# Output rows of one batch of an attention and routing kernel: transposed by DMA instead of on TensorE

## The chip, the core and the metric

One core of a Trainium2 chip runs the whole kernel. The metric is device time in microseconds (us). The core has five engines with instruction streams of their own, each worked through in order: TensorE (PE in the rows; its weight loads are listed apart as PEld), VectorE (DVE), ScalarE (ACT), GpSimd (POOL) and SyncE (SP). Engines wait for one another by semaphores. 16 DMA engines move data between HBM and SBUF, and can also move it from SBUF to SBUF.

## The reference

```python
# q, k, v: (8, 12, 448, 64) float32
scores = (1 / sqrt(64)) * q @ k.T
attn   = maximum(scores, 0) ** 2 / 448
x      = (attn @ v), heads side by side: (8, 448, 768)
# then, for each of the 8 batches
s   = x[b] @ w_gate                       # 448 scores
top = the 128 rows with the highest s
ye  = maximum(x[b, top] @ w1, 0) @ w2     # w1: 768 x 1024, w2: 1024 x 768
out[b]      = x[b]
out[b, top] = x[b, top] + sigmoid(s[top]) * ye
```

## The kernel before

The work comes in 24 units: unit u is the group of four heads u % 3 of batch u // 3, so units 12, 13 and 14 are the fifth batch (b = 4). The order of all instructions is written out by hand, in a long string of items (`ORDER`, lines 525 to 621); each engine gets its instructions in the order in which the items stand. An item is a letter code with its arguments. For one unit:

- `T` transposes q and k of the unit on TensorE, `TE` copies the result out of PSUM.
- `S(u, c, at)` computes a score step: four matmuls of 448 columns into the pair of PSUM banks `at`, `at + 1` (banks 0 and 1, or 2 and 3). Two such items often stand together; the text calls them a score pair. `R` (line 251) is the relu that empties the two banks, most on ScalarE, some on VectorE. `Q` squares on VectorE.
- `V` multiplies by v and sums up in another pair of banks, `X` (line 283) scales the sum into `xT_sb`, the output of the unit with features on partitions and positions along the row.
- `RT` (line 288) turns it round: eight 128x128 transposes on TensorE into one PSUM bank. `RE` (line 298) copies that bank into `x_sb`, the rows in output order.

For one batch: `G`, `bc`, `col` and `colE` compute the gate scores from `xT_sb`, `rk` and `cs` rank them, `ri` makes the ranks integers, and four `sc` (line 386) scatter the rows of `x_sb` by rank into a buffer in HBM. `rb` (line 397) reads the first 128 of them back as `xe`, `xt` transposes them, `h` and `y` are the two matrix products, `ADD` adds the result to the output. `ST` (line 313) stores all rows of `x_sb`. Scatters, stores and the loads of q, k and v (`Lq`, `Lk`, `Lv`) are issued by GpSimd and share one queue; `rb` is issued by SP.

There are two buffers of `xT_sb` (batches take turns) and three of `x_sb`. The banks 4 to 7 are shared by `T`, `V`, `RT`, `G`, `h`, `y` and the rest. The function `XB` (line 304) stands in the kernel before, and no item of the order uses it. What surrounds the changed items in the order, at line 578: `S,16,2,2 RT,13,5 cs,3,4 S,16,6,0 ... S,16,3,2 X,14,6,D G,4,0,7`, and from there `xt,2,6 ... RT,14,4 ... S,17,2,0 S,16,1,2`, then `RT,12,6 ... h,2,0,4 ... S,16,4,0 ... S,16,5,2`.

Of the kernel before, what the change touches and what calls it, by code (L numbers as in the profile page):

```python
# [23 lines left out]
def kernel(  # L24
# [557 lines left out]
    R,17,4,2,A T,18,6,0 T,18,6,1 h,2,6,5 h,2,7,5 y,2,1,0,4 Q,15,0 S,17,1,0 hE,2,1,5,A TE,18,6,2,D S,17,0,2
    R,17,1,0,A y,2,1,2,4 T,19,6,0 Q,17,1 R,17,0,2,A y,2,0,0,5 y,2,1,4,4 Q,16,2 y,2,1,6,4 T,19,6,1 TE,19,6,2,D
    S,18,5,0 S,17,5,2 R,18,5,0,A yE,2,1,4 y,2,0,2,5 R,17,5,2,A y,2,0,4,5 y,2,0,6,5 sc,3,1 S,17,6,0 col,4,4
    V,15,0,6 S,18,0,2 ST,2,1 V,15,1,6 V,15,2,6 R,17,6,0,A yE,2,0,5 Q,17,0 V,15,3,6 S,19,0,0 V,15,4,6 sc,3,0
    colE,4,4 R,18,0,2,A sc,3,2 V,15,5,6 V,15,6,6 S,18,2,2 V,17,0,4 R,19,0,0,A V,17,1,4 V,17,2,4 X,15,6,A
    V,17,3,4 Q,17,2 S,18,1,0 V,17,4,4 R,18,2,2,D V,17,5,4 V,17,6,4 V,16,0,6 V,16,1,6 R,18,1,0,A ST,2,0 V,16,2,6
    X,17,4,A S,18,3,2 Lv,6,0,6 V,16,3,6 S,18,4,0 R,18,3,2,A V,16,4,6 ADD,2 V,16,5,6 V,16,6,6 rk,4,0 rk,4,1
    rk,4,3 Lq,7,0,6 R,18,4,0,D T,20,4,0 Lk,7,0,6 X,16,6,A rb,3 T,20,4,1 S,18,6,2 S,19,6,0 rk,4,2 G,5,0,6
    R,18,6,2,A G,5,1,6 TE,20,4,2,D G,5,2,6 R,19,6,0,A xt,3,4 S,19,1,2 ST,3,1 Q,18,0 S,19,5,0 bc,5,6,A R,19,1,2,A  # L590
    ix,3 xtE,3,4,D Q,18,2 RT,17,5 R,19,5,0,A cs,4,4 RT,16,6 ri,4,4 RE,16,6,A col,5,7 S,19,4,2 S,19,2,0 Q,19,0
    R,19,2,0,A h,3,0,4 h,3,1,4 h,3,2,4 colE,5,7 V,18,0,6 Q,18,1 S,19,3,0 R,19,4,2,A V,18,1,6 RE,17,5,D V,18,2,6
    V,18,3,6 S,20,5,2 R,19,3,0,A V,18,4,6 rk,5,0 V,18,5,6 V,18,6,6 R,20,5,2,A S,20,0,0 R,20,0,0,A h,3,3,4
    h,3,4,5 hE,3,0,4,A Q,19,2 h,3,5,5 h,3,6,5 sc,4,2 S,20,4,0 rk,5,3 S,20,3,2 y,3,1,0,4 X,18,6,A Q,19,1 h,3,7,5
    T,21,6,0 T,21,6,1 R,20,4,0,A R,20,3,2,D hE,3,1,5,A S,20,2,0 S,20,1,2 y,3,1,2,4 TE,21,6,2,D sc,4,1 RT,15,5
    sig,3 R,20,2,0,A V,19,0,6 S,21,4,0 V,19,1,6 R,20,1,2,A rk,5,2 V,19,2,6 sc,4,0 V,19,3,6 rk,5,1 V,19,4,6
    RE,15,5,D sc,4,3 V,19,5,6 R,21,4,0,A V,19,6,6 X,19,6,A S,20,6,2 S,21,1,0 ST,4,1 cs,5,5 Q,20,1 y,3,1,4,4
    ri,5,5 ST,3,0 T,22,6,0 T,22,6,1 R,21,1,0,A Q,20,0 R,20,6,2,A S,21,6,0 R,21,6,0,A y,3,0,0,5 TE,22,6,2,D
    y,3,1,6,4 y,3,0,2,5 Q,20,2 y,3,0,4,5 S,22,0,2 S,21,0,0 V,20,0,6 R,22,0,2,A V,20,1,6 V,20,2,6 yE,3,1,4
    R,21,0,0,A V,20,3,6 V,20,4,6 rb,4 V,20,5,6 S,21,2,2 R,21,2,2,A Lv,7,0,6 V,20,6,6 sc,5,2 RT,18,4 y,3,0,6,5  # L600
    X,20,6,D yE,3,0,5 S,21,3,0 Q,21,0 S,22,6,2 T,23,6,0 RE,18,4,A T,23,6,1 sc,5,0 G,6,0,5 R,21,3,0,A G,6,1,5
    R,22,6,2,A G,6,2,5 xt,4,4 bc,6,5,A TE,23,6,2,D S,22,1,2 S,22,2,0 col,6,5 ix,4 xtE,4,4,D h,4,4,7 colE,6,5
    RT,20,4 R,22,1,2,A rk,6,1 h,4,5,7 R,22,2,0,A rk,6,2 rk,6,0 RT,19,5 sig,4 sc,5,1 S,22,3,2 RE,20,4,A RE,19,5,D
    S,21,5,0 h,4,6,7 rk,6,3 h,4,7,7 cs,6,4 sc,5,3 R,21,5,0,A h,4,0,5 h,4,1,5 hE,4,1,7,A R,22,3,2,A Q,21,1
    h,4,2,5 h,4,3,5 ADD,3 S,22,4,0 S,23,2,2 V,21,0,6 hE,4,0,5,A V,21,1,6 ri,6,4 R,23,2,2,A V,21,2,6 Q,21,2
    V,21,3,6 V,21,4,6 V,21,5,6 V,21,6,6 R,22,4,0,D S,22,5,0 R,22,5,0,A S,23,3,2 R,23,3,2,A Q,22,1 y,4,1,0,4
    y,4,1,2,4 y,4,0,0,5 Q,22,0 y,4,1,4,4 X,21,6,A y,4,1,6,4 S,23,4,0 R,23,4,0,A S,23,0,2 ST,4,0 y,4,0,2,5 Zl
    y,4,0,4,5 rb,5 y,4,0,6,5 RT,21,6 xt,5,7 Q,22,2 S,23,1,0 sc,6,0 R,23,0,2,A S,23,5,2 sc,6,3 yE,4,1,4 yE,4,0,5
    RE,21,6,D V,22,0,4 V,22,1,4 ix,5 xtE,5,7,D V,22,2,4 V,22,3,4 Q,23,1 V,22,4,4 V,22,5,4 R,23,1,0,A sc,6,2
    V,22,6,4 S,23,6,0 h,5,4,7 R,23,5,2,A sc,6,1 h,5,0,6 R,23,6,0,A h,5,1,6 Q,23,0 h,5,2,6 h,5,3,6 X,22,4,A  # L610
    h,5,5,7 V,23,0,2 Q,23,2 V,23,1,2 hE,5,0,6,D V,23,2,2 V,23,3,2 V,23,4,2 V,23,5,2 V,23,6,2 ADD,4 G,7,0,6
    RT,22,5 h,5,6,7 G,7,1,6 ST,6,0 X,23,2,A RE,22,5,A G,7,2,6 bc,7,6,A h,5,7,7 RT,23,1 ST,6,1 y,5,0,0,4
    hE,5,1,7,A RE,23,1,A col,7,6 y,5,0,2,4 rb,6 colE,7,6 rk,7,0 y,5,1,0,6 y,5,1,2,6 y,5,1,4,6 y,5,0,4,4
    y,5,0,6,4 rk,7,1 hot,7,1 hot,7,0 y,5,1,6,6 xt,6,7 rk,7,3 sig,5 xg,7,0,0 xg,7,1,0 rk,7,2 hot,7,2 hot,7,3
    xg,7,2,0 xg,7,3,0 ix,6 xtE,6,7,A h,6,0,5 ST,5,0 xgE,7,1,0,A yE,5,1,6 yE,5,0,4 h,6,1,5 h,6,2,5 h,6,3,5
    h,6,4,2 xgE,7,0,0,A h,6,5,2 hE,6,0,5,A p,7,0 p,7,1 h,6,6,2 p,7,2 p,7,3 sel,7,7 ST,5,1 ST,7,0,0,512
    ST,7,1,0,512 ST,7,0,512,768 ST,7,1,512,768 h,6,7,2 sE,7,0,7 sE,7,1,-1 sE,7,2,-1 sgl,7 y,6,1,0,0 y,6,1,2,0
    ADD,5 xr,7 hE,6,1,2,D y,6,1,4,0 y,6,1,6,0 sig,6 h,7,0,4 h,7,4,1 yE,6,1,0 h,7,5,1 h,7,1,4 h,7,2,4 h,7,3,4
    h,7,6,1 h,7,7,1 hE,7,0,4,D hE,7,1,1,A y,6,0,0,6 y,6,0,2,6 y,6,0,4,6 y,6,0,6,6 yE,6,0,6 ADD,6 y,7,1,0,2
    y,7,0,0,4 y,7,0,2,4 y,7,1,2,2 y,7,0,4,4 y,7,0,6,4 y,7,1,4,2 yE,7,0,4 y,7,1,6,2 yE,7,1,2 ADD,7  # L620
# [53 lines left out]
```

## Time and profile before

| | |
|---|---|
| median of 3 runs | 205.4 us (205.3 to 205.61) |
| profiled execution | 204.92 us, of which the span 203.2 us |
| TensorE busy | 188.6 us (93%) |
| VectorE busy | 173.2 us (85%) |
| ScalarE busy | 166.6 us (82%) |
| GpSimd busy | 108.9 us (54%) |
| TensorE's granted clock, mean | 0.999 |

The shares are over the whole span. The engine times are time with an instruction in it; register work, waits and the issuing of DMAs by SP don't count. A busy TensorE need not be at its peak, since matmuls are pipelined and their ends are modelled.

### The profile page before, as it was taken

How to read it: one execution, taken by the hardware profiler on the slowest of the kernel's cores; microseconds unless marked ns; L12 is line 12 of the kernel's file. 1: busy time of each engine (PE TensorE's matmuls, PEld its weight loads, DVE VectorE, ACT ScalarE, POOL GpSimd, SP SyncE). 2: the span in 40 equal slices, each digit the busy share in tenths (PEclk: the TensorE clock that was granted, in tenths of full speed). 3: DMA queues.
4: the chain of work that ended last, by engine and by line, in shares of the span. 5: the costliest groups of instructions: out<-in, count | busy, mean ns of one | idle time of the engine just before them, and what ended most of it. 6: DMA issues, size and time to landing. Idle time of an engine off the chain costs nothing.

```text
span 203.2 us, 6985 instructions
## 1 busy us (share of the span) xinstructions
PE 188.6 (93%) x3028; PEld 120.9 (59%) x3028; DVE 173.2 (85%) x274; ACT 166.6 (82%) x216; POOL 108.9 (54%) x133
## 2 busy tenths in 40 slices
...
GB/s 185 180 203 202 205 204 204 206 214 121 16 92 220 206 211 151 280 219 230 52 338 203 125 65 221 222 231 183 210 301 175 130 162 18 75 391 412 175 65 155
DMA packets 28970, 37.89 MB, mean 186 GB/s; under 512 B 2523, under 2 KB 23813, under 8 KB 28940
## 3 DMA queue, kind: packets, MB, share of 16 engines
q0 software_dynamic: 27344, 35.15, 84.1%
...
q8 instruction: 23, 0.38, 0.7%
q10 hardware_dynamic: 288, 0.46, 0.6%
...
## 4 chain that ended last, share of the span: by engine, by line
PE 60%; ACT 25%; issue 6%; DVE 4%; DMA 2%; POOL 1%; POOLq 1%; ACTq 0%; DVEq 0%
PE banks L215 34%; ACT r_sb L275 23%; PE banks L247 14%; PE banks L268 11%; DMA kf<-in_k_dram 2%; ACT xT_sb L275 2%; DVE mk L359 1%; PE banks L343 1%; POOLq L669 1%; DVE qkt L279 1%; DVE a_sb L260 1%; PE banks L154 1%; POOL q_sb L478 1%; POOL out_dram L514 0%; ACT bc_sb L275 0%
## 5 line engine op out<-in xcount | busy, mean ns | idle before, releaser
L275 ACT ACTIVATE r_sb<-banks 128x896 bf16<-128x896 f32 x155 | 132.9, 950 | 12.1 <-PE banks L247 9.4
L260 DVE TENSOR_TENSOR a_sb<-r_sb 128x1792 bf16<-128x1792 bf16 (+1 forms) x72 | 87.4, 1238 | 0.3 <-ACT r_sb L275 0.2
L386 POOL DMA_INDIRECT xe_dram<-x_sb,rank_i x28 | 41.4, 1478 | 51.5 <-DVE rank_i L382 37.8
L247 PE MATMUL banks<-qkt 64*64 64x448 bf16 x672 | 58.4, 363 | 6.5 <-ACT r_sb L275 4.8
L268 PE MATMUL banks<-a_sb,v_sb 64*64 64x448 bf16 x672 | 43.6, 351 | 0.0
L247 PEld LDWEIGHTS <-qkt 64*64 64x64 bf16 x672 | 22.6, 104 | 29.6 <-issue 18.3
L279 DVE COPY qkt<-banks 128x1792 bf16<-128x1792 bf16 (+1 forms) x25 | 26.2, 1050 | 4.8 <-PE banks L215 3.4
L268 PEld LDWEIGHTS <-v_sb 64*64 64x64 bf16 x672 | 21.1, 106 | 9.5 <-issue 1.2
L215 PE MATMUL banks<-xeT,w_sb 128*128 128x128 bf16 x384 | 25.4, 219 | 0.5 <-DVE xeT L279 0.5
L514 POOL DMA_INDIRECT out_dram<-orow,idx x7 | 10.8, 1540 | 27.0 <-DVE orow L509 16.3
L215 PE MATMUL banks<-w_sb,hT 128*128 128x384 bf16 x128 | 24.6, 327 | 0.2 <-DVE hT L277 0.2
L215 PEld LDWEIGHTS <-w_sb 128*128 128x128 bf16 x384 | 22.0, 98 | 4.0 <-issue 3.4
L275 ACT ACTIVATE xT_sb<-banks 128x896 bf16<-128x896 f32 x19 | 18.0, 948 | 2.4 <-PE banks L268 2.4
L277 DVE TENSOR_SCALAR r_sb<-banks 128x896 bf16<-128x896 f32 x13 | 14.1, 1088 | 3.8 <-PE banks L247 2.4
L215 PEld LDWEIGHTS <-hT 128*128 128x128 bf16 x128 | 10.9, 98 | 10.3 <-issue 3.6
L359 DVE SCALAR_TENSOR_TENSOR mk<-bc_sb,x_sb,tie 128x448 bf16<-128x448 f32 (+4 forms) x32 | 15.2, 501 | 0.2
L215 PE MATMUL banks<-ident,xT_sb 128*128 128x128 bf16 x192 | 14.8, 220 | 0.2 <-ACT xT_sb L275 0.2
L215 PE MATMUL banks<-ident,k_sb 128*64 128x128 bf16 x336 | 14.0, 221 | 0.2 <-ACT k_sb L275 0.2
L215 PE MATMUL banks<-ident,q_sb 128*64 128x128 bf16 x336 | 14.0, 222 | 0.1
L215 PEld LDWEIGHTS <-xT_sb 128*128 128x128 bf16 x192 | 11.4, 98 | 4.2 <-issue 2.5
L215 PEld LDWEIGHTS <-q_sb 128*64 128x64 bf16 x336 | 10.3, 109 | 5.8 <-issue 5.0
L313 POOL DMA_DIRECT2D out_dram<-x_sb x18 | 12.1, 679 | 2.1 <-ACT x_sb L275 1.4
...
## 6 DMA issues: line engine op xcount, KB each, us to landing
...
```

Source lines behind the costliest of these rows:

```text
L154: nc.tensor.matmul(out=banks[col:col + 64, at + x, :S], lhsT=zero[lo:lo + 64, 0:64], rhs=zero[lo:lo + 64, :], start=True, stop=True, skip_ ...
L215: nc.tensor.matmul(out=out, lhsT=lhsT, rhs=rhs, start=start, stop=stop, skip_group_check=True, **kw)
L247: nc.tensor.matmul(out=banks[col:col + 64, at + x, :S], lhsT=sb[lo:lo + 64, 1, c, hh, :], rhs=sb[lo:lo + 64, 0, :, hh, :], start=True, sto ...
L260: nc.vector.tensor_tensor(out=a, in0=r, in1=r, op=ALU.mult)
L268: nc.tensor.matmul(out=banks[col:col + 64, at + x, :S], lhsT=vs[lo:lo + 64, 2 * i + x, c, :], rhs=a[lo:lo + 64, c - SLOTS[g][0], x, :], st ...
L275: nc.scalar.activation(out=out_, in_=in_, func=func or AF.Copy, scale=scale)
L277: nc.vector.tensor_scalar(out=out_, in0=in_, scalar1=0.0, scalar2=None, op0=ALU.max)
L279: nc.vector.tensor_copy(out=out_, in_=in_)
L313: nc.gpsimd.dma_start(out=rows, in_=x_rows[b % NROW][64 * cp:64 * cp + 64, 0:NJ - cp, c0:c1])
L359: nc.vector.scalar_tensor_tensor(out=dst, in0=self.bc_[:n, t0:S], scalar=self.cols[:n, j:j + 1], in1=tie[:n, j, t0:], op0=ALU.subtract, op ...
L386: done = nc.gpsimd.indirect_dma_start(out=xe_dram[self.b][:, :], out_offset=bass.IndirectOffsetOnAxis(ap=self.rank_i[:, j:j + 1], axis=0), ...
L514: done = nc.gpsimd.indirect_dma_start(out=out[0:self.b + 1].rearrange("b s d -> (b s) d"), out_offset=bass.IndirectOffsetOnAxis(ap=self.id ...
```

## The change

The three `RT` items and the three `RE` items of units 12, 13 and 14 go. In the place of each `RT` stands the item `XB` of the same unit. `XB` issues two DMAs on SP, one for each half of the unit's 256 features: each reads 128 partitions x 512 bf16 of `xT_sb` and writes, transposed, 128 columns of the four blocks of rows in `x_sb`. The rest of the order is word for word the same, and only its line breaks differ. Cut to its core:

```diff
-    R,15,1,0,A V,14,6,6 S,16,2,2 RT,13,5 cs,3,4 S,16,6,0 Q,15,1 R,16,2,2,A S,16,3,2 X,14,6,D G,4,0,7 R,16,6,0,A
-    xt,2,6 R,16,3,2,A ri,3,4 RT,14,4 Q,15,2 G,4,1,7 S,17,2,0 S,16,1,2 ix,2 xtE,2,6,A R,16,1,2,A G,4,2,7 bc,4,7,A
-    RT,12,6 sc,3,3 RE,14,4,D h,2,0,4 sig,2 R,17,2,0,D S,16,4,0 RE,13,5,D Q,16,1 RE,12,6,D R,16,4,0,A S,16,5,2
...
+    R,15,1,0,A V,14,6,6 S,16,2,2 XB,13 cs,3,4 S,16,6,0 Q,15,1 R,16,2,2,A S,16,3,2 X,14,6,D G,4,0,7 R,16,6,0,A
+    xt,2,6 R,16,3,2,A ri,3,4 XB,14 Q,15,2 G,4,1,7 S,17,2,0 S,16,1,2 ix,2 xtE,2,6,A R,16,1,2,A G,4,2,7 bc,4,7,A
+    XB,12 sc,3,3 h,2,0,4 sig,2 R,17,2,0,D S,16,4,0 Q,16,1 R,16,4,0,A S,16,5,2 h,2,1,4 h,2,2,4 h,2,4,5 h,2,3,4
...
```

The function that the new items call, there before and after:

```python
    def XB(u):
        b, i = divmod(u, NU)
        for m in (2 * i, 2 * i + 1):
            nc.sync.dma_start_transpose(
                out=x_rows[b % NROW][:, :, m * 128:(m + 1) * 128],
                in_=xT_sb[b % NX][:, m, :, :].rearrange("r c p -> r (c p)"))
```

SP's stream around the new DMAs, `-` before and `+` after. `xT_sb0` and `x_sb1` are the buffers of the fifth batch, `xe_dram2` to `xe_dram6` the scattered rows of the third to the seventh batch:

```order
 L397 DMA xe_1967<-xe_dram1_103 128x386
 L397 DMA xe_2211<-xe_dram2_104 128x386
-L397 DMA xe_2858<-xe_dram3_105 128x386
-L397 DMA xe_3291<-xe_dram4_106 128x386
-L397 DMA xe_3592<-xe_dram5_107 128x386
-L397 DMA xe_3801<-xe_dram6_108 128x386
+L307 DMA_TRANSPOSE x_sb1_93<-xT_sb0_90 128x4x128 x6
+L397 DMA xe_2837<-xe_dram3_105 128x386
+L397 DMA xe_3270<-xe_dram4_106 128x386
+L397 DMA xe_3571<-xe_dram5_107 128x386
+L397 DMA xe_3780<-xe_dram6_108 128x386
```

All six transposes stand ahead of the read of the fourth batch's `xe`; the other reads keep their order.

VectorE's stream of before, from the squaring ahead of the removed copies to the copy of the next unit's q and k (`a_sb` is a squaring, `r_sb` a relu, `qkt` the copy of q and k):

```order
L260 TENSOR_TENSOR a_sb2_2465<-r_sb2_2256 128x2688
L410 COPY idx_2477<-xe_2211 128x1
L279 COPY x_sb1_93<-banks_101 128x4x256
L277 TENSOR_SCALAR r_sb1_2505<-banks_101 128x896
L279 COPY x_sb1_93<-banks_101 128x4x256
L260 TENSOR_TENSOR a_sb1_2512<-r_sb1_2437 128x1792
L279 COPY x_sb1_93<-banks_101 128x4x256
L260 TENSOR_TENSOR a_sb0_2561<-r_sb0_2393 128x1792
L260 TENSOR_TENSOR a_sb0_2611<-r_sb0_2313 128x1792
L279 COPY qkt_2618<-banks_101 128x1792
```

And the same place of VectorE's stream after:

```order
L260 TENSOR_TENSOR a_sb2_2453<-r_sb2_2256 128x2688
L410 COPY idx_2465<-xe_2211 128x1
L277 TENSOR_SCALAR r_sb1_2486<-banks_101 128x896
L260 TENSOR_TENSOR a_sb1_2492<-r_sb1_2431 128x1792
L260 TENSOR_TENSOR a_sb0_2540<-r_sb0_2393 128x1792
L260 TENSOR_TENSOR a_sb0_2590<-r_sb0_2313 128x1792
L279 COPY qkt_2597<-banks_101 128x1792
```

The relu into `r_sb1` follows `idx` directly, and three squarings follow it without a copy between them. On TensorE the 24 transposes are gone and nothing else has moved.

## Rows read from the trace of the kernel before

**Rows 1.** The page's chain that ended last, by engine

```profile
PE 60%; ACT 25%; issue 6%; DVE 4%; DMA 2%; POOL 1%; POOLq 1%; ACTq 0%; DVEq 0%
```

**Rows 2.** Stretches: length, busy time by engine, granted clock, DMA share, GB/s

```profile
113.00:121.00 8.00, 7.99 (x129) 5.24 (x122) 7.54 (x11) 7.65 (x12) 5.94 (x7) 1.00 0.33 74
121.00:125.00 4.00, 4.00 (x74) 2.55 (x70) 3.99 (x5) 3.70 (x6) 3.39 (x4) 1.00 1.28 261
```

**Rows 3.** TensorE's waits, 100 to 170 us: total, times, longest

```profile
PE banks L247 <- issue: 0.7, 2, 0.5
```

**Rows 4.** Order in time, TensorE's weight loads: start, us, what [idle before]

```profile
115.65 0.11 PEld L247 LDWEIGHTS <-qkt 64*64 64x64 bf16 x3 [0.27 <-issue]
```

**Rows 5.** Order in time, ScalarE, 111 to 128 us

```profile
111.44 6.02 ACT L275 ACTIVATE r_sb<-banks 128x896 bf16<-128x896 f32 x7 [1.11 <-PE banks L247]
...
114.67 0.93 ACT L275 ACTIVATE r_sb<-banks 128x896 bf16<-128x896 f32 x1
...
117.35 0.82 ACT L275 ACTIVATE xeT<-banks 128x768 bf16<-128x768 bf16 x1
118.23 0.92 ACT L275 ACTIVATE r_sb<-banks 128x896 bf16<-128x896 f32 x1
...
127.69 0.92 ACT L275 ACTIVATE r_sb<-banks 128x896 bf16<-128x896 f32 x1 [1.36 <-PE banks L247]
```

**Rows 6.** Order in time, TensorE's matmuls, 115 to 130 us

```profile
115.26 0.78 PE L247 MATMUL banks<-qkt 64*64 64x448 bf16 x8
...
117.61 0.57 PE L247 MATMUL banks<-qkt 64*64 64x448 bf16 x8
118.11 0.55 PE L215 MATMUL banks<-xT_sb,wg_col 128*128 128x448 bf16 x2
118.50 0.61 PE L215 MATMUL banks<-ident,xT_sb 128*128 128x128 bf16 x8
118.95 0.50 PE L215 MATMUL banks<-xeT,w_sb 128*128 128x128 bf16 x6
119.38 0.38 PE L247 MATMUL banks<-qkt 64*64 64x448 bf16 x4
...
127.21 0.57 PE L247 MATMUL banks<-qkt 64*64 64x448 bf16 x8
...
129.44 0.38 PE L268 MATMUL banks<-a_sb,v_sb 64*64 64x448 bf16 x4
```

**Rows 7.** Order in time, VectorE, from 117 us

```profile
117.34 0.69 DVE L279 COPY x_sb<-banks 128x1024 bf16<-128x1024 bf16 x1
118.10 1.09 DVE L277 TENSOR_SCALAR r_sb<-banks 128x896 bf16<-128x896 f32 x1
```

**Rows 8.** Order in time: the copies into xT_sb of units 13 and 14

```profile
106.53 0.92 ACT L275 ACTIVATE xT_sb<-banks 128x896 bf16<-128x896 f32 x1 [0.22 <-PE banks L268]
...
114.53 1.09 DVE L281 TENSOR_SCALAR xT_sb<-banks 128x896 bf16<-128x896 f32 x1 [0.28 <-PE banks L268]
```

**Rows 9.** Order in time: DMAs issued by GpSimd and by SP

```profile
118.05 0.85 POOL L115 DMA_DIRECT2D v_sb<-in_v_dram  x1
...
127.87 0.32 SPq L397 DMA_DIRECT2D xe<-xe_dram  x1
...
140.20 1.65 POOL L386 DMA_INDIRECT xe_dram<-x_sb,rank_i  x1 [4.80 <-DVE rank_i L382]
```

**Rows 10.** Stretches with stores at the end, and where the v load lands

```profile
123.00:124.00 1.00, 1.00 (x20) 0.78 (x14) 0.99 (x2) 1.00 (x3) 1.00 (x1) 1.00 1.27 229
124.00:125.00 1.00, 1.00 (x12) 0.26 (x10) 1.00 (x2) 0.94 (x2) 0.70 (x2) 1.00 1.29 406
...
181.00:184.00 3.00, 3.00 (x28) 1.89 (x26) 1.59 (x6) 1.82 (x4) 2.24 (x4) 1.00 1.33 423
```

**Rows 11.** DMA queues: packets, MB, packet time as share of 16 engines' span

```profile
q0 software_dynamic: 27344, 35.15, 84.1%
q10 hardware_dynamic: 288, 0.46, 0.6%
```

More of the change, by code (lines that the diff above doesn't have):

```diff
@@ L577 @@
     V,14,0,6 yE,1,0,5 V,14,1,6 Lk,6,0,6 Lq,6,0,6 V,14,2,6 ADD,1 S,15,1,0 R,16,0,2,A V,14,3,6 V,14,4,6 V,14,5,6
-    R,15,1,0,A V,14,6,6 S,16,2,2 RT,13,5 cs,3,4 S,16,6,0 Q,15,1 R,16,2,2,A S,16,3,2 X,14,6,D G,4,0,7 R,16,6,0,A
-    xt,2,6 R,16,3,2,A ri,3,4 RT,14,4 Q,15,2 G,4,1,7 S,17,2,0 S,16,1,2 ix,2 xtE,2,6,A R,16,1,2,A G,4,2,7 bc,4,7,A
-    RT,12,6 sc,3,3 RE,14,4,D h,2,0,4 sig,2 R,17,2,0,D S,16,4,0 RE,13,5,D Q,16,1 RE,12,6,D R,16,4,0,A S,16,5,2
-    h,2,1,4 h,2,2,4 h,2,4,5 h,2,3,4 h,2,5,5 S,17,3,0 R,16,5,2,A hE,2,0,4,A S,17,4,2 Q,16,0 Lv,5,0,6 R,17,3,0,A
@@ L582 @@
[L582 to L620, printed above, removed]
+    R,15,1,0,A V,14,6,6 S,16,2,2 XB,13 cs,3,4 S,16,6,0 Q,15,1 R,16,2,2,A S,16,3,2 X,14,6,D G,4,0,7 R,16,6,0,A
@@ new lines @@
+    xt,2,6 R,16,3,2,A ri,3,4 XB,14 Q,15,2 G,4,1,7 S,17,2,0 S,16,1,2 ix,2 xtE,2,6,A R,16,1,2,A G,4,2,7 bc,4,7,A
+    XB,12 sc,3,3 h,2,0,4 sig,2 R,17,2,0,D S,16,4,0 Q,16,1 R,16,4,0,A S,16,5,2 h,2,1,4 h,2,2,4 h,2,4,5 h,2,3,4
+    h,2,5,5 S,17,3,0 R,16,5,2,A hE,2,0,4,A S,17,4,2 Q,16,0 Lv,5,0,6 R,17,3,0,A R,17,4,2,A T,18,6,0 T,18,6,1
+    h,2,6,5 h,2,7,5 y,2,1,0,4 Q,15,0 S,17,1,0 hE,2,1,5,A TE,18,6,2,D S,17,0,2 R,17,1,0,A y,2,1,2,4 T,19,6,0
+    Q,17,1 R,17,0,2,A y,2,0,0,5 y,2,1,4,4 Q,16,2 y,2,1,6,4 T,19,6,1 TE,19,6,2,D S,18,5,0 S,17,5,2 R,18,5,0,A
@@ new lines @@
+    yE,2,1,4 y,2,0,2,5 R,17,5,2,A y,2,0,4,5 y,2,0,6,5 sc,3,1 S,17,6,0 col,4,4 V,15,0,6 S,18,0,2 ST,2,1 V,15,1,6
+    V,15,2,6 R,17,6,0,A yE,2,0,5 Q,17,0 V,15,3,6 S,19,0,0 V,15,4,6 sc,3,0 colE,4,4 R,18,0,2,A sc,3,2 V,15,5,6
+    V,15,6,6 S,18,2,2 V,17,0,4 R,19,0,0,A V,17,1,4 V,17,2,4 X,15,6,A V,17,3,4 Q,17,2 S,18,1,0 V,17,4,4
+    R,18,2,2,D V,17,5,4 V,17,6,4 V,16,0,6 V,16,1,6 R,18,1,0,A ST,2,0 V,16,2,6 X,17,4,A S,18,3,2 Lv,6,0,6
+    V,16,3,6 S,18,4,0 R,18,3,2,A V,16,4,6 ADD,2 V,16,5,6 V,16,6,6 rk,4,0 rk,4,1 rk,4,3 Lq,7,0,6 R,18,4,0,D
@@ new lines @@
+    T,20,4,0 Lk,7,0,6 X,16,6,A rb,3 T,20,4,1 S,18,6,2 S,19,6,0 rk,4,2 G,5,0,6 R,18,6,2,A G,5,1,6 TE,20,4,2,D
+    G,5,2,6 R,19,6,0,A xt,3,4 S,19,1,2 ST,3,1 Q,18,0 S,19,5,0 bc,5,6,A R,19,1,2,A ix,3 xtE,3,4,D Q,18,2 RT,17,5
+    R,19,5,0,A cs,4,4 RT,16,6 ri,4,4 RE,16,6,A col,5,7 S,19,4,2 S,19,2,0 Q,19,0 R,19,2,0,A h,3,0,4 h,3,1,4
+    h,3,2,4 colE,5,7 V,18,0,6 Q,18,1 S,19,3,0 R,19,4,2,A V,18,1,6 RE,17,5,D V,18,2,6 V,18,3,6 S,20,5,2
+    R,19,3,0,A V,18,4,6 rk,5,0 V,18,5,6 V,18,6,6 R,20,5,2,A S,20,0,0 R,20,0,0,A h,3,3,4 h,3,4,5 hE,3,0,4,A
@@ new lines @@
+    Q,19,2 h,3,5,5 h,3,6,5 sc,4,2 S,20,4,0 rk,5,3 S,20,3,2 y,3,1,0,4 X,18,6,A Q,19,1 h,3,7,5 T,21,6,0 T,21,6,1
+    R,20,4,0,A R,20,3,2,D hE,3,1,5,A S,20,2,0 S,20,1,2 y,3,1,2,4 TE,21,6,2,D sc,4,1 RT,15,5 sig,3 R,20,2,0,A
+    V,19,0,6 S,21,4,0 V,19,1,6 R,20,1,2,A rk,5,2 V,19,2,6 sc,4,0 V,19,3,6 rk,5,1 V,19,4,6 RE,15,5,D sc,4,3
+    V,19,5,6 R,21,4,0,A V,19,6,6 X,19,6,A S,20,6,2 S,21,1,0 ST,4,1 cs,5,5 Q,20,1 y,3,1,4,4 ri,5,5 ST,3,0
+    T,22,6,0 T,22,6,1 R,21,1,0,A Q,20,0 R,20,6,2,A S,21,6,0 R,21,6,0,A y,3,0,0,5 TE,22,6,2,D y,3,1,6,4 y,3,0,2,5
@@ new lines @@
+    Q,20,2 y,3,0,4,5 S,22,0,2 S,21,0,0 V,20,0,6 R,22,0,2,A V,20,1,6 V,20,2,6 yE,3,1,4 R,21,0,0,A V,20,3,6
+    V,20,4,6 rb,4 V,20,5,6 S,21,2,2 R,21,2,2,A Lv,7,0,6 V,20,6,6 sc,5,2 RT,18,4 y,3,0,6,5 X,20,6,D yE,3,0,5
+    S,21,3,0 Q,21,0 S,22,6,2 T,23,6,0 RE,18,4,A T,23,6,1 sc,5,0 G,6,0,5 R,21,3,0,A G,6,1,5 R,22,6,2,A G,6,2,5
+    xt,4,4 bc,6,5,A TE,23,6,2,D S,22,1,2 S,22,2,0 col,6,5 ix,4 xtE,4,4,D h,4,4,7 colE,6,5 RT,20,4 R,22,1,2,A
+    rk,6,1 h,4,5,7 R,22,2,0,A rk,6,2 rk,6,0 RT,19,5 sig,4 sc,5,1 S,22,3,2 RE,20,4,A RE,19,5,D S,21,5,0 h,4,6,7
@@ new lines @@
+    rk,6,3 h,4,7,7 cs,6,4 sc,5,3 R,21,5,0,A h,4,0,5 h,4,1,5 hE,4,1,7,A R,22,3,2,A Q,21,1 h,4,2,5 h,4,3,5 ADD,3
+    S,22,4,0 S,23,2,2 V,21,0,6 hE,4,0,5,A V,21,1,6 ri,6,4 R,23,2,2,A V,21,2,6 Q,21,2 V,21,3,6 V,21,4,6 V,21,5,6
+    V,21,6,6 R,22,4,0,D S,22,5,0 R,22,5,0,A S,23,3,2 R,23,3,2,A Q,22,1 y,4,1,0,4 y,4,1,2,4 y,4,0,0,5 Q,22,0
+    y,4,1,4,4 X,21,6,A y,4,1,6,4 S,23,4,0 R,23,4,0,A S,23,0,2 ST,4,0 y,4,0,2,5 Zl y,4,0,4,5 rb,5 y,4,0,6,5
+    RT,21,6 xt,5,7 Q,22,2 S,23,1,0 sc,6,0 R,23,0,2,A S,23,5,2 sc,6,3 yE,4,1,4 yE,4,0,5 RE,21,6,D V,22,0,4
```

12 lines of the change are left out of this document (added).

## The prediction

> **What bounds the kernel now.** I read the page first, then the stages, then the one stage that the change touches. The chain that ended last runs mainly over TensorE (60%) and ScalarE (25%) [rows 1]: look for two engines that take turns, so that neither alone sets the time. Next the time in stretches: from 113 to 121 us, where the three transposes of units 12 to 14 stand, TensorE is busy 7.99 of 8 us, VectorE 7.54 and ScalarE 7.65, while the DMA share is 0.33 against 1.28 in the four microseconds behind [rows 2]. Three engines are full, the DMA engines are mostly free. The list of waits, taken from 100 to 170 us, has only 0.7 us for TensorE's matmuls [rows 3]. That looks like a pure TensorE bound, by which every removed matmul would come back in full. The order in time says something narrower, and the forecast rests on it: TensorE's weight loads stop for 0.27 us inside a pair of score steps, until 115.65 [rows 4], and the second step follows the end of a ScalarE relu at 114.67 + 0.93 = 115.60 [rows 5]. A score step writes a pair of banks that a relu has to empty first. So TensorE here is early enough to run into ScalarE, and its "busy" hides that.
>
> **What goes.** Each RT is 8 matmuls. From the start of RT(12) to that of the next item is 118.95 - 118.50 = 0.45 us [rows 6]; three such are 1.35 us of TensorE. Each RE is one VectorE copy of 0.69 us [rows 7], three of them 2.07 us. Nothing goes from ScalarE: all three RE were on VectorE.
>
> **What of it reaches the end.** I walk the stage with the durations of before and ask at each place what is late next.
> - RT(13) stood before the score pair at 115.26 [rows 6]. The second half of this pair waited for ScalarE already; without RT(13) it waits 0.45 us longer. Gain at 115.65: nothing.
> - RT(14) stood before the pair at 117.61 [rows 6]. Its second half ran at 117.61 + 0.25 = 117.86 (half of the 0.50 us from a pair to the next item); it needs the bank pair of the last of seven relus that run without a gap from 111.44 to 111.44 + 6.02 = 117.46 [rows 5]. With the 0.05 us of latency seen above it can start at 117.50: gain 0.36, and 0.09 is lost.
> - ScalarE then has the copy of xeT, 117.35 + 0.82 = 118.17, and the relu that began at 118.23 [rows 5]. Its step would be ready at 117.50 + 0.38 = 117.88 (0.38 from the first matmul of a step to its end), so the relu starts when ScalarE is free, about 118.09 (relus in a row overlap by some 0.08): gain 0.14, end 118.09 + 0.92 = 119.01.
> - RT(12) stood before the first h group, which also needs xeT (118.17). It can start at 118.22 instead of 118.95; h takes 119.38 - 118.95 = 0.43 [rows 6], to 118.65. The score pair behind it, 119.38 before, needs two banks. The first is emptied by VectorE's relu, which began at 118.10 behind an RE [rows 7]; with that RE gone and its score step 0.45 earlier it starts at about 117.6 and ends at 118.7. The second needs the ScalarE relu that ends at 119.01: it starts at 119.06, where before it stood at 119.38 + 0.25 = 119.63. Gain 0.57.
> - Behind that TensorE has h groups, transposes and y groups, and ScalarE, which has its next relus some 0.3 earlier. At the next pairs the relus end just before TensorE comes, so 0.57 stays. At 127.69 ScalarE had stood idle for 1.36 us waiting for the pair at 127.21 [rows 5, 6]; it now starts 0.57 earlier. From here on TensorE, VectorE and ScalarE wait for one another alone and shift together.
>
> So of the 1.35 us some 0.8 goes to ScalarE's pace and 0.57 comes through. VectorE's 2.07 us are off the path: at 119 to 127 us it would only stand idle longer before the next transposes of TensorE.
>
> **What is added.** Six transposing DMAs of 128 x 512 bf16, 131 KB each and 0.79 MB in all, queued on SP, with three costs.
> - Start. The first pair (unit 13) needs ScalarE's copy that ends at 106.53 + 0.92 = 107.45; the second (unit 14) the VectorE copy that ends at 114.53 + 1.09 = 115.62 [rows 8]; the third pair (unit 12) is queued behind it, though its data are older. SP has nothing else until the read of xe for the fourth batch, issued at 127.87 [rows 9]. That gives four transposes 12 us on SP before anything queued behind them is late.
> - Landing. The first to wait for all six is GpSimd's scatter at 140.20 [rows 9], 24.6 us after the start of the second pair. Behind it GpSimd holds later scatters, stores and loads; nothing is late if six land in that time.
> - Engine time. The trace has no such transfer. By bytes it is 0.79 MB at the 423 GB/s of the stores near the end = 1.9 us of all engines, at the 261 GB/s of 121 to 125 us [rows 2, 10] 3.0 us. By packets: if each 256-byte output row (128 elements) were a packet, 3072 of them, at 0.006 x 16 x 203.2 / 288 = 0.068 us (queue 10) to 0.841 x 16 x 203.2 / 27344 = 0.100 us (queue 0) [rows 11], over 16 engines 13 to 19 us. I take 3 us, the row of the same stretch, and keep 1.9 and 19. From 113 to 121 the engines have (1.28 - 0.33) x 8 / 1.28 = 5.9 us to spare [rows 2], which hides 3 us. Below nothing it cannot be: a transfer added frees no engine beyond what is counted above.
>
> The row shows spare engines and no duration. [...]
>
> Sum: the profiled execution took 204.92 us, its span 203.2 and 1.7 around it; 204.92 - 0.57 = 204.35. The median of the runs is 205.4, 0.48 higher; on it the change gives 204.8.
>
> **Rivals.**
> - *All of TensorE's time comes back.* If ScalarE's relus move forward with TensorE (the order of start times allows it only if I misread which bank each step waits for), the gain is 1.35 us: 204.05. For it: the list of waits. Against it: the stop at 115.65.
> - *Nothing comes back.* The 0.57 us is lost again between 127 and 190 us, at a relu, a scatter or a load whose time is not tied to these engines: 205.4, within 0.3. For it: ScalarE and VectorE are nearly as full as TensorE, and the length of GpSimd's scatters changes from one to the next. Against: TensorE shows no wait for a DMA there.
> - *The transposes hold up the loads: slower.* The v rows of the sixth batch are loaded from about 119 us [rows 9]; the step from 229 to 406 GB/s, where a store follows, says that they have landed by about 124.2 [rows 10]; their first matmul is at 129.44 [rows 6], 128.87 with the gain. Spare engine time 5.9 + 4.6 us of slack = 10.5 us: from there on each microsecond of transposes stalls TensorE by one, if they go first. At 13 us that is 2.5 - 0.57 = +1.9 (207.3), at 19 us +7.9 (213.3). For it: no row bounds a transposing packet. Against: by bytes it is 3 us.
>
> **How the numbers follow.** Forecast 0.42 (its own range 204.4 to 205.2), all of it 0.15, nothing 0.23, slower 0.20. About 0.2% (0.41 us) is what a measurement of this kernel can tell from no change. The forecast's centre lies just beyond it, so three quarters of its chance count as faster: 0.42 x 0.75 + 0.15 = 0.46 faster; the rest of it and the second rival, less some for its lower edge, 0.32 same; 0.22 slower. The range goes from a little below the full gain, 203.9, to 207.0, which takes in the small end of the slow rival and leaves out its large end.
>
> **What would show it.** Right: the score pair's second half still stops near 115.65, the one of 119.63 comes near 119.06, ScalarE's relu of 127.69 starts near 127.1, and the scatter at 140.20 starts about 0.6 earlier, ended by VectorE's rank and not by a DMA. Wrong upward: ScalarE's seven relus end before 117.4. Wrong downward: TensorE waits for the v load near 129, ScalarE for a DMA before its later copies into xT, or SP issues the read of xe after 128.

## The result, and the profile after

| | before | after |
|---|---|---|
| median of 4 runs each | 205.47 us (205.3 to 205.61) | 207.12 us (205.96 to 207.39) |
| ratio, 95% interval | | 1.0064 (1.0038 to 1.0090): slower |
| profiled execution / span | 204.92 / 203.2 us | 205.96 / 204.1 us |
| TensorE busy | 188.6 us | 187.7 us |

The ratio is an estimate over the executions and not the quotient of the two medians (1.0080). With nine more runs of the changed kernel, in the first series of experiments below, it was 1.0086 (1.0050 to 1.0123). The prediction was 204.8 us, with 0.22 on slower and 207.0 as the upper end. Executions more than 1.5% above their kernel's fastest are left out of every ratio: nine of twelve in the experiment on the seventh batch, one or two in e8, e9a and e9b, one of the kernel before in the third series, none elsewhere.

The page of the changed kernel: the chain that ended last by engine, and the two DMA queues that matter.

```profile
PE 47%; ACT 22%; DMA 12%; issue 8%; DVE 6%; POOL 2%; POOLq 1%; ACTq 0%
...
q0 software_dynamic: 27344, 35.15, 86.3%
q1 hardware_dynamic: 4572, 2.63, 6.7%
```

DMAs now have 12% of the chain, where they had 2% [rows 1]; half of the 12% is the load of the last batch's k. Queue 1 is SP's; before, its line was:

```profile
q1 hardware_dynamic: 1308, 1.85, 3.6%
```

The six transposes are 4572 - 1308 = 3264 packets and 2.63 - 1.85 = 0.78 MB, some 240 bytes a packet.

TensorE's matmuls of the changed kernel, in order of time (start, us, what, and in brackets the idle time before it and what ended it):

```profile
113.65 0.36 PE L247 MATMUL banks<-qkt 64*64 64x448 bf16 x4
...
115.04 0.38 PE L247 MATMUL banks<-qkt 64*64 64x448 bf16 x4 [0.43 <-ACT r_sb L275]
116.55 0.57 PE L247 MATMUL banks<-qkt 64*64 64x448 bf16 x8
118.19 0.57 PE L247 MATMUL banks<-qkt 64*64 64x448 bf16 x8 [0.25 <-DVE r_sb L277]
...
126.02 0.57 PE L247 MATMUL banks<-qkt 64*64 64x448 bf16 x8
...
137.37 0.51 PE L215 MATMUL banks<-ident,xe 128*128 128x128 bf16 x6 [0.93 <-DMA xe<-xe_dram]
...
147.79 0.58 PE L215 MATMUL banks<-ident,k_sb 128*64 128x128 bf16 x14 [0.53 <-DMA k_sb<-in_k_dram]
```

And in the kernel before, the row from which I count, and the last two of the same places, which waited for nothing:

```profile
114.26 0.36 PE L247 MATMUL banks<-qkt 64*64 64x448 bf16 x4
...
137.22 0.50 PE L215 MATMUL banks<-ident,xe 128*128 128x128 bf16 x6
...
146.96 0.58 PE L215 MATMUL banks<-ident,k_sb 128*64 128x128 bf16 x14
```

The two executions differ by 0.61 us at the first of these rows, the score step of unit 16 ahead of the removed work. So I count from there. To the score pair of 127.21 [rows 6] it was 12.95 us and is 126.02 - 113.65 = 12.37: a gain of 0.58. To the transposes of `xe` it was 22.96 and is 23.72; to those of the last k it was 32.70 and is 34.14. The gain is made, and lost again at two waits for DMAs.

SP and then GpSimd of the changed kernel, in order of time:

```profile
107.00 14.39 SPq L307 DMA_TRANSPOSE x_sb<-xT_sb  x6
131.74 0.33 SPq L397 DMA_DIRECT2D xe<-xe_dram  x1
```
```profile
123.40 1.64 POOL L386 DMA_INDIRECT xe_dram<-x_sb,rank_i  x1 [0.30 <-issue]
125.02 0.73 POOL L313 DMA_DIRECT2D out_dram<-x_sb  x1
...
133.92 1.03 POOL L514 DMA_INDIRECT out_dram<-orow,idx  x1 [4.32 <-DVE mk L359]
...
134.99 0.88 POOL L108 DMA_DIRECT2D q_sb<-in_q_dram  x1
135.83 0.87 POOL L111 DMA_DIRECT2D k_sb<-in_k_dram  x1
...
140.29 1.65 POOL L386 DMA_INDIRECT xe_dram<-x_sb,rank_i  x1 [2.97 <-DVE rank_i L382]
```

The same two places of GpSimd before:

```profile
124.61 1.77 POOL L386 DMA_INDIRECT xe_dram<-x_sb,rank_i  x1 [0.30 <-issue]
...
131.07 1.96 POOL L514 DMA_INDIRECT out_dram<-orow,idx  x1 [1.95 <-DVE x_sb L349]
...
133.89 0.88 POOL L111 DMA_DIRECT2D k_sb<-in_k_dram  x1
```

- The read of `xe` of the fourth batch waits until the batch's scatters have landed: SP's list of waits has 10.2 us for it here, 8.7 of it in one piece. Before, it was issued 127.87 - 124.61 = 3.3 us after the start of the last scatter [rows 9]; now 131.74 - 123.40 = 8.3 us after. SP itself had issued its last transpose by 107.00 + 14.39 = 121.39, so it is not SP that was late. The transposes of `xe` are the first wait, 0.93 us.
- The add of the third batch (L514) writes rows that the third batch's stores have written, and so is ordered behind them. The profile puts the 4.32 us of idle time down to VectorE, but that row (the ranking) is not an input of the add, whose own was written by 127.14 + 1.26 = 128.40 us (first row below). That leaves the DMAs of queue 0: the stores, which the profile of e5 below names at this place (2.7 us), or another transfer of the queue, which is not excluded (the v load at 128.98, which needs no store, also stood 1.33 us behind the DMA of an earlier load). The add came 2.85 us later than before (3.46 counted from the score step), and the last loads of q and k stand behind it on GpSimd. The transposes of k are the second wait, 0.53 us here and 1.53 us in the other profile of this kernel. The chain that ended last goes this way: over the add to the load of k, which took 11.92 us from its issue.
- The scatter at 140.29, the first place at which the prediction had anything wait for all six, is still ended by VectorE's rank.

The add's input on VectorE, and two pieces of the chain (start, us, what), all of the changed kernel:

```profile
127.14 1.26 DVE L509 SCALAR_TENSOR_TENSOR orow<-banks,g__2484,xe 128x384 f32<-128x384 f32 x2
```
```profile
133.92 0.25 POOL out_dram L514
...
135.83 11.92 DMA k_sb<-in_k_dram
```

What filled the queue, by stretch. First 121 to 128 us of before, then of after (packets, MB, and the time from start to end of all packets as a share of 16 engines; shares pass 100% here, so packets of one queue overlap, and this time is more than the engines' own work):

```profile
q0 software_dynamic: 1138, 1.48, 93.0%
```
```profile
q0 software_dynamic: 712, 0.63, 114.4%
q1 hardware_dynamic: 1044, 0.25, 33.3%
```

Queue 0, with all scatters, stores and loads of GpSimd, moved 712 packets where it had moved 1138, with a third of the transposes still under way beside it.

### The profile page after: what moved, and what is told of

Read it like the earlier page. It is cut to its first block, busy times and chain, and to the rows that moved or that the text cites. A ratio compares the mean times of both kernels' runs of the same rounds, so it can differ in the third digit from the quotient of the medians.

```text
span 204.1 us, 6948 instructions
## 1 busy us (share of the span) xinstructions
PE 187.7 (92%) x3004; PEld 120.5 (59%) x3004; DVE 171.6 (84%) x271; ACT 166.6 (82%) x216; POOL 105.7 (52%) x133
## 3 DMA queue, kind: packets, MB, share of 16 engines
q1 hardware_dynamic: 4572, 2.63, 6.7%
## 4 chain that ended last, share of the span: by engine, by line
PE 47%; ACT 22%; DMA 12%; issue 8%; DVE 6%; POOL 2%; POOLq 1%; ACTq 0%
PE banks L215 26%; ACT r_sb L275 20%; PE banks L247 12%; PE banks L268 9%; DMA k_sb<-in_k_dram 6%; DMA out_dram<-x_sb 3%; DMA q_sb<-in_q_dram 3%; DVE a_sb L260 3%; ACT xT_sb L275 1%; DVE qkt L279 1%; DVE r_sb L277 1%; DVE mk L359 1%; POOL out_dram L514 1%; POOLq L669 1%; POOL q_sb L478 1%
## 5 line engine op out<-in xcount | busy, mean ns | idle before, releaser
L386 POOL DMA_INDIRECT xe_dram<-x_sb,rank_i x28 | 39.7, 1418 | 50.8 <-DVE rank_i L382 37.4
L247 PE MATMUL banks<-qkt 64*64 64x448 bf16 x672 | 59.3, 364 | 6.7 <-ACT r_sb L275 5.0
L247 PEld LDWEIGHTS <-qkt 64*64 64x64 bf16 x672 | 23.4, 104 | 29.5 <-issue 18.1
L268 PEld LDWEIGHTS <-v_sb 64*64 64x64 bf16 x672 | 22.5, 106 | 8.9 <-issue 1.5
L514 POOL DMA_INDIRECT out_dram<-orow,idx x7 | 9.9, 1409 | 28.4 <-DVE orow L509 15.4
L118 POOL DMA_DIRECT2D v_sb<-in_v_dram x20 | 12.1, 614 | 4.0 <-DMA v_sb<-in_v_dram 1.3
L215 PE MATMUL banks<-ident,xT_sb 128*128 128x128 bf16 x168 | 12.9, 220 | 0.2 <-ACT xT_sb L275 0.2
```

The lines of the kernel that those rows point to most:

```text
L118: nc.gpsimd.dma_start(out=t[rows, p0 + 1:p1:2], in_=half_heads(v, b, p0 + 1, p1, hh))
L215: nc.tensor.matmul(out=out, lhsT=lhsT, rhs=rhs, start=start, stop=stop, skip_group_check=True, **kw)
L247: nc.tensor.matmul(out=banks[col:col + 64, at + x, :S], lhsT=sb[lo:lo + 64, 1, c, hh, :], rhs=sb[lo:lo + 64, 0, :, hh, :], start=True, sto ...
L268: nc.tensor.matmul(out=banks[col:col + 64, at + x, :S], lhsT=vs[lo:lo + 64, 2 * i + x, c, :], rhs=a[lo:lo + 64, c - SLOTS[g][0], x, :], st ...
L386: done = nc.gpsimd.indirect_dma_start(out=xe_dram[self.b][:, :], out_offset=bass.IndirectOffsetOnAxis(ap=self.rank_i[:, j:j + 1], axis=0), ...
L514: done = nc.gpsimd.indirect_dma_start(out=out[0:self.b + 1].rearrange("b s d -> (b s) d"), out_offset=bass.IndirectOffsetOnAxis(ap=self.id ...
```

## The experiments

The theory: the removal is worth what was forecast, and the transposes take so long in the DMA engines that they run into the scatters and stores of 121 to 128 us. Rivals: the number of small packets does it, whatever they carry; or the removal itself shifts the engines so that the loads come too late.

Three series, each kernel beside the kernel before on the same chip (first: 205.33 us; second: 204.51; third: 204.64). The expectations give times as on the first chip; in the second and third series the ratios decide. The distances are counted as above, from the score step of unit 16 in each profiled execution, and worked out from start times:

| kernel | median, us | ratio (95%) | to the pair of unit 18 | to `xe` | to the last k | to the end |
|---|---|---|---|---|---|---|
| before | 205.33 | 1 | 12.95 | 22.96 | 32.70 | 88.94 |
| after (result above) | 207.12 | 1.0064 (1.0038-1.0090) | 12.37 | 23.72 | 34.14 | 90.45 |
| after, again | 206.71 | 1.0086 (1.0050-1.0123) | 12.37 | 23.21 | 34.62 | 91.28 |
| e1 removal alone | 204.99 | 0.9988 (0.9959-1.0017) | 12.37 | 22.39 | 32.12 | 88.66 |
| e3 plain, 1 KB | 204.63 | 0.9979 (0.9950-1.0007) | 12.36 | 22.38 | 32.10 | 88.40 |
| e4 plain, 256 B | 205.01 | 0.9991 (0.9967-1.0015) | 12.37 | 22.38 | 32.12 | 88.69 |
| e8 loads first | 205.10 | 1.0049 (1.0026-1.0072) | 12.37 | 22.65 | 32.37 | 88.64 |
| e5 pairs early | 204.04 | 0.9989 (0.9965-1.0013) | 12.38 | 22.39 | 32.06 | 88.20 |
| e5 again | 204.45 | 0.9981 (0.9956-1.0005) | 12.37 | 22.39 | 32.10 | 88.59 |

**e1: the removal alone.** The six transposes are left out, so the fifth batch's output rows are not written into `x_sb`.

```diff
-... S,16,2,2 XB,13 cs,3,4 ... ri,3,4 XB,14 Q,15,2 ... XB,12 sc,3,3 ...
+... S,16,2,2 cs,3,4 ... ri,3,4 Q,15,2 ... sc,3,3 ...
```

> The TensorE transposes and evictions of units 12 to 14 are gone and nothing stands in their place, so the output rows of the fifth batch are left out. Theory (the transposing DMAs slow the shared DMA engines, and TensorE later waits for loads and for xe): the 0.57 us of the walk arrives and is kept, 204.6 to 205.1, and TensorE waits for no DMA between 100 and 170 us. Rival (the removal itself upsets the take-turns of TensorE, ScalarE and VectorE): still 206 to 207.4, as with the change.

The distances show 0.58 us gained at the pair of unit 18 and kept as far as the last k: 0.57 at `xe`, 0.58 at k. To the end of the span 0.28 is left in this execution, and 0.25 to 0.74 in those of e3, e4 and e5. TensorE waits for no DMA between 100 and 170 us. In the medians 0.34 us is inside the interval. The rival that the removal does the harm falls. Measured against e1, the changed kernel loses 1.33 us up to `xe` and 2.02 us up to k.

**e3 and e4: the same bytes without transposing.** Plain copies from `xT_sb` to `x_sb`, at the same places and on the same queue; the output rows of the batch are not turned round. e4 copies 256-byte pieces (4476 - 1308 = 3168 packets), e3 1 KB and 512-byte pieces (1120 packets). The edit shown is that of e4.

```diff
-            nc.sync.dma_start_transpose(
-                out=x_rows[b % NROW][:, :, m * 128:(m + 1) * 128],
-                in_=xT_sb[b % NX][:, m, :, :].rearrange("r c p -> r (c p)"))
+            nc.sync.dma_start(out=x_rows[b % NROW][:, :, m * 128:(m + 1) * 128],
+                              in_=xT_sb[b % NX][:, m, :, :].rearrange("r (j c) p -> r j (c p)", j=NJ))
```

> As before but the plain copies write pieces of 256 B, some 3072 packets; the rows come out untransposed. If the number of packets is what costs: 206 to 207.4, as with the change, and xe of the fourth batch is again read some 4 us late. If it is the transposing itself that costs: as with the 1 KB copies, 204.7 to 205.6.

> The six transposing DMAs are replaced by plain copies of the same bytes from the same tile on the same queue at the same places, in pieces of 1 KB (four of them) and 512 B (two), some 1024 packets instead of 3264; the rows come out untransposed. Theory, by packets: a third of the packets, so most of the loss goes, 204.7 to 205.6. Rival, by bytes (or by merely having six more DMAs on SP): 206 to 207.4, as with the change.

Neither loses anything. So it is not the packets' number or size by itself. But both are early: e4 has no packet of its copies left in 121 to 128 us, and e3 had issued its last by 117.07 + 1.26 = 118.33. What plain packets would cost beside the scatters there, they don't show. e4's queue 1 on the page, and behind it the times from issue to landing of its six copies:

```profile
q1 hardware_dynamic: 4476, 2.63, 5.5%
```
```profile
DMA to landing us min/median/max: 2.4/2.7/3.1
```

And of the changed kernel's six transposes, time on SP (ns each, min/median/max) and to landing:

```profile
L307 SPq DMA_TRANSPOSE x_sb<-xT_sb x6: 1264/1420/2195, 107.0 to 119.3; - x6
DMA to landing us min/median/max: 3.8/8.0/11.0
```

With the 3.6% of 203.2 us of before taken off, e4's copies took 0.055 x 203.1 - 7.3 = 3.9 us of the 16 engines, by the time of their packets. The transposes took 0.067 x 204.1 - 7.3 = 6.4 us here, and in the other profile (7.9% of 204.9 us) 8.9 us.

**After, again.** The changed kernel in the first of the three series, to have it beside e1, e3 and e4.

> The change itself, beside the others on one chip: its four runs were 205.96 to 207.39, wide apart. Theory: 206 to 207.4 again, and where it is slow TensorE waits longer for the q and k of the last batch and for xe of the fourth. Rival (the first runs were chance): within 0.2% of before, 205.4.

The loss came again, and larger at k:

```profile
136.83 0.51 PE L215 MATMUL banks<-ident,xe 128*128 128x128 bf16 x6 [0.67 <-DMA xe<-xe_dram]
...
148.24 0.58 PE L215 MATMUL banks<-ident,k_sb 128*64 128x128 bf16 x14 [1.53 <-DMA k_sb<-in_k_dram]
```

**e9a and e9b: which of them.** The same change with the transposes of unit 13 alone, and with those of units 14 and 12 alone; the others are left out.

```diff
-... XB,13 cs,3,4 ... ri,3,4 XB,14 Q,15,2 ... XB,12 sc,3,3 ...
+... XB,13 cs,3,4 ... ri,3,4 Q,15,2 ... sc,3,3 ...
```

and

```diff
-... XB,13 cs,3,4 ... ri,3,4 XB,14 Q,15,2 ... XB,12 sc,3,3 ...
+... cs,3,4 ... ri,3,4 XB,14 Q,15,2 ... XB,12 sc,3,3 ...
```

> The change with only the two transposes of unit 13, which start at 107 us beside the loads of the seventh batch's q and k; those of units 14 and 12 are left out, with their output rows. Theory: these loads have 9 us of slack, so no loss against the removal alone: 204.6 to 205.3, xe issued near 128. Rival (each pair costs a third of the loss): 205.4 to 205.9.

> The change with only the four transposes of units 14 and 12, which start at 115 us and later; those of unit 13 are left out, with its output rows. Theory: these four collide with the v load and the scatters, so nearly all of the loss is here: 206.0 to 207.2, xe issued near 131. Rival (each pair costs a third): 205.7 to 206.4, xe near 130.

e9a: 204.13 us, 0.9981 (0.9961 to 1.0001). e9b: 205.51 us, 1.0051 (1.0028 to 1.0074). The four that start last carry the loss; that each pair costs a third falls with e9a. Where e9b's time goes can't be shown: the profiled execution was its fastest (203.03 us), with 0.2 us of waiting for `xe` by the weight loads and none for k. Its read of `xe` came 129.30 - 112.93 = 16.4 us after the score step, between the 18.1 of the change and the 14.4 of e5. Its queue 1 took 38.9% of 121 to 128 us, about as in the changed kernel, so transposes in that stretch don't cost the same in every execution.

**e5: the same six, earlier.** Unit 12's data are older than unit 13's. The four DMAs of these two units are queued right behind the store that reads the buffer's old rows; unit 14's two stay in place.

```diff
-... S,16,0,2 ST,1,0 R,15,6,0,A ... S,16,2,2 XB,13 cs,3,4 ... XB,12 sc,3,3 ...
+... S,16,0,2 ST,1,0 XB,12 XB,13 R,15,6,0,A ... S,16,2,2 cs,3,4 ... sc,3,3 ...
```

> The change, with the transposes of unit 12 issued right behind the stores of the second batch and ahead of unit 13, so that four transposes run from 107 us and two from 115. Theory (what costs is transposes beside the v load and the scatters from 119 us): the transposes are over by about 121, xe is issued within 1.5 us of 127.9, 205.0 to 205.8. Rival (the number of transposes costs, wherever they lie in this stage): 206.3 to 207.4.

SP's rows of e5, and its queues from 113 to 121 us and from 121 to 128 us:

```profile
107.80 10.86 SPq L307 DMA_TRANSPOSE x_sb<-xT_sb  x6
128.38 0.32 SPq L397 DMA_DIRECT2D xe<-xe_dram  x1
```
```profile
q1 hardware_dynamic: 3073, 0.75, 95.1%
q0 software_dynamic: 350, 0.59, 36.2%
...
q0 software_dynamic: 1398, 1.97, 118.8%
...
q1 hardware_dynamic: 33, 0.00, 0.6%
```

The list of waits of e5, 100 to 170 us, has one for a DMA on GpSimd's add:

```profile
POOL out_dram L514 <- DMA out_dram<-x_sb: 2.7, 1, 2.7
```

Here the profile names what the add waits for, the stores, and they land in time. The transposes are all but through by 121 us (33 packets are left). Queue 0 moves 1398 packets behind them, `xe` is read at 128.38, and TensorE waits for no DMA: all that the change lost is back, with the same six transposes. From 113 to 121 us 3073 of their packets took 0.951 x 8 = 7.6 us, 8.1 for all 3264. The two profiles of the changed kernel have 6.4 and 8.9: where the transposes lie decides here, and not what they take. A second run of e5 in the third series:

> The change with unit 12's transposes ahead of unit 13's, once more, since the first comparison left open whether it is faster than before. Theory (0.57 us arrives and nothing is given back): ratio to before 0.996 to 0.999. Rival (transposes always give something back): 1.000 to 1.003.

The ratios are 0.9989 and 0.9981, both intervals with 1 in them: as good as the removal alone, better than the change, and not shown to be faster than before.

**e8: the loads ahead of the add.** In the changed kernel the last loads of q and k are issued before the third batch's add. e8b is the same move in the kernel before.

```diff
-... V,16,4,6 ADD,2 V,16,5,6 ... Lq,7,0,6 R,18,4,0,D T,20,4,0 Lk,7,0,6 X,16,6,A ...
+... V,16,4,6 Lq,7,0,6 Lk,7,0,6 ADD,2 V,16,5,6 ... R,18,4,0,D T,20,4,0 X,16,6,A ...
```

> The change, with the loads of q and k of the last batch issued by GpSimd ahead of the third batch's add instead of behind it. Theory (the transposes delay the stores, the add waits for these, and the loads stand behind the add; TensorE then waits for k): TensorE's wait for k of 0.5 to 1.5 us goes and the wait for xe of 0.7 to 1.4 us stays, 205.3 to 206.2. Rival (the wait for k comes from engine time alone, wherever the loads stand): no better than the change, 206.3 to 207.4.

> The kernel before with the loads of the last batch's q and k ahead of the third batch's add, as a control of the experiment that did this in the change. Theory (TensorE waits for no load in the kernel before): ratio 0.998 to 1.002. Rival (the order of the loads costs or gains by itself): outside of that.

In the profiled execution the wait for k goes (the load of k is issued at 129.33 instead of 135.83), and that for `xe` stays (0.5 us of the weight loads). So the place behind the late add is what made k late. The price of this path stays open: 1.0049 is below the change's two ratios, but the intervals overlap, and by the ratio the result lies as well in the rival's range. The profiled execution is also the fastest of the twelve (203.91 us), so what the others lost is not shown. e8b is 0.9999 (0.9974 to 1.0023); the move alone is worth nothing.

**e6: one unit of the three.** The kernel before, with only unit 12 transposed by DMA, behind `ST,1,0`.

```diff
-... ST,1,0 R,15,6,0,A ... RT,12,6 sc,3,3 RE,14,4,D ... Q,16,1 RE,12,6,D R,16,4,0,A ...
+... ST,1,0 XB,12 R,15,6,0,A ... sc,3,3 RE,14,4,D ... Q,16,1 R,16,4,0,A ...
```

> The kernel before with only unit 12 by transposing DMAs, issued behind the second batch's stores at 107 us; units 13 and 14 stay on TensorE and VectorE. Theory (RT(13) gives nothing, RT(14) and RT(12) give the 0.57 us between them; two early transposes cost nothing): the score pair of unit 18 comes 0.3 to 0.5 us nearer to the one of unit 16, ratio 0.997 to 0.9995. Rival (only all three together free the path): no change in that distance, ratio 0.999 to 1.001.

The expectation failed: the pair of unit 18 comes 13.46 us after the score step, 0.51 later than before, and the time is 204.99 us, 1.0023 (0.9995 to 1.0051). The pair before it still stood 124.02 - 114.25 = 9.77 us behind the score step, against 124.17 - 114.26 = 9.91: a gain of 0.14, and not of 0.3 to 0.5. The loss behind that is on the engines, in one place of ScalarE:

```profile
122.01 1.73 ACT L275 ACTIVATE r_sb<-banks 128x896 bf16<-128x896 f32 x2
125.48 0.60 ACT L275 ACTIVATE hT<-banks 128x512 bf16<-128x512 f32 x1 [1.74 <-PE banks L247]
```

This copy began at 123.95 before. The last h matmuls ahead of it ended at 122.92 + 0.84 = 123.76, and at 123.91 before. Why it starts 1.7 us behind them here is not settled, and so e6 doesn't tell what two early transposes cost.

**e7: the same idea at another place.** The kernel before, with units 18 to 20 (the seventh batch) by transposing DMAs, `RT` and `RE` of these units gone.

```diff
-... ri,5,5 ST,3,0 T,22,6,0 ... RT,18,4 ... X,20,6,D yE,3,0,5 ... RE,18,4,A ... RT,20,4 ... RT,19,5 ... RE,20,4,A RE,19,5,D
+... ri,5,5 ST,3,0 XB,18 XB,19 T,22,6,0 ... X,20,6,D XB,20 yE,3,0,5 ...
```

> The kernel before with the output rows of the seventh batch (units 18 to 20) by transposing DMAs in place of those of the fifth; two of their evictions were on ScalarE, so 2.1 us of ScalarE go too. The transposes start near 150 us, the last pair near 158, and the scatters of this batch begin at 166. Theory (they cost only where loads or scatters are needed soon, and take about 8 us of the engines in all): the last pair lands just in time, ratio 0.995 to 0.999, GpSimd's scatter still ended by the rank. Rival: the scatter or the read of the sixth batch's xe waits for the transposes, ratio 1.000 to 1.008.

By its ratio, 1.0010 (0.9957 to 1.0062) from three runs, it is inconclusive. The median of all twelve is 207.73 us, against 204.64 for the kernel before, and whether that is the edit's doing is not decided. The profiled execution took 209.59 us, so it is used for the order of SP's work alone:

```profile
152.38 5.89 SPq L307 DMA_TRANSPOSE x_sb<-xT_sb  x4
158.50 0.39 SPq L397 DMA_DIRECT2D xe<-xe_dram  x1
```

The read of the fifth batch's `xe`, issued at 148.79 in the kernel before, stood behind four transposes on SP, and TensorE then waited 2.54 us for it; what that wait would be in an execution of 204 us is not shown.

## Why the prediction was wrong

- **The gain was right in size and in kind, and its last digit was luck.** 0.57 us forecast, 0.58 measured in both profiles of the change and in e1; 0.57 to 0.59 in the plain copies and e5. The pair's second half still stops at the same distance: 115.04 + 0.61 = 115.65 [rows 4], now with 0.43 us put down to ScalarE. The score pair of 119.38 [rows 6] now begins at 118.19 + 0.61 = 118.80, and so its second half at 118.80 + 0.25 = 119.05 (forecast 119.06). But ScalarE's seven relus ended earlier than I had it (110.83 + 5.78 + 0.61 = 117.22 instead of 117.46), which I had named as a sign of more gain. The pair behind RT(14) came the full 0.45 us earlier and not 0.36, and ScalarE's next relu ended at 117.18 + 0.95 + 0.61 = 118.74 instead of 119.01. No more came of it, because VectorE's relu, at 117.05 + 1.09 + 0.61 = 118.75 (forecast 118.7), was then the last: the pair's recorded wait is for it, and not for ScalarE. The two rows of the changed kernel:

```profile
117.18 0.95 ACT L275 ACTIVATE r_sb<-banks 128x896 bf16<-128x896 f32 x1
...
117.05 1.09 DVE L277 TENSOR_SCALAR r_sb<-banks 128x896 bf16<-128x896 f32 x1 [0.43 <-ACT r_sb L275]
```

  That VectorE's 2.07 us give nothing beyond this was right, and e1 shows that the gain is kept to the last k where no transposes are.
- **"I take 3 us, the row of the same stretch" failed.** By the time of their packets the transposes took 6.4, 8.9 and 8.1 us of the engines. The rows of 121 to 125 us (3.0 us) and of the stores (1.9 us) did not price these transposing DMAs, and neither does their packet count: plain copies of nearly as many packets (3168 against 3264) took 3.9 us. The bounds of 1.9 and 19 held it; the choice inside them went by bytes, to the low end. This alone would not have turned the sign: e5 pays 8.1 us and loses nothing.
- **"The first to wait for all six is GpSimd's scatter at 140.20" was right and beside the point; this step turned the sign.** I looked for who waits for the transposes, and not for who shares the engines with them. By my own sum, 5.9 + 4.6 us of room, 8 to 9 us would still have been hidden, because I kept one deadline there, the v load. Those that broke were the fourth batch's scatters (the read of `xe`) and the third batch's stores (its add, and the loads behind it on GpSimd). I had the read of `xe` in the list only as an item of SP's queue, with 12 us to spare there; what made it late was its data. The sign that I had named for it, a read issued after 128 us, came (131.74).
- **The window.** I set all six against the spare time from 113 to 121 us, but those of units 14 and 12 could not start before 113.92 + 1.09 = 115.01, the end of VectorE's copy. So 1044 packets were left behind 121 us, in the stretch with little room (queue 0 alone had 93.0% there before); e5, which queues unit 12's pair first and has four queued from 107.8 us, has 33 there and loses nothing.
- **The slow rival** was right in kind: the transposes held up transfers that TensorE then waited for (0.93 us for `xe`, 0.53 for k). Its place was wrong (the v load came in time), and so was the point from which it decides (10.5 us).
- What isn't shown: by packet time the transposes took 0.333 x 7 = 2.3 us of the engines in 121 to 128 us, and the read of `xe` came 131.74 - 113.65 = 18.1 us after the score step, against 128.38 - 114.00 = 14.4 in e5. The other 1.4 us, why queue 0's packets took longer beside the transposes (1.144 x 16 x 7 / 712 = 0.180 us on the mean in 121 to 128 us, against 0.930 x 16 x 7 / 1138 = 0.092 before), whether plain packets in their place would have done the same, and what makes the loss vary from one execution to the next, no run here settles.

For all six together 0.79 MB in e5's 8.1 us of packet time is 97 GB/s, where the forecast took 261, and the plain copies of e4 took half the time. The mean time of a packet was not the same in every run, as the last section shows.
